# Turning the first batch's attention weights by TensorE's transpose mode, with x^T divided instead, and converting the float64 weights from one load

## The chip, the cores and the metric

The kernel runs on one core of a Trainium2 chip. The metric is the device time of one execution in microseconds (us). Seven runs of the kernel before gave a median of 1355.04 us, the lowest 1353.45 and the highest 1357.39.

## The reference: what is computed

Thresholded attention over 8 batches of 8 heads, 576 positions and head width 64, followed by a two-layer MLP with the exact gelu:

```python
scores = scale * np.matmul(q, k.transpose(0, 1, 3, 2))
thresh = np.max(scores, axis=-1, keepdims=True) - tau
scores = np.where(scores >= thresh, scores, -1000000000.0)
attn = np.exp(scores - np.max(scores, axis=-1, keepdims=True))
attn = attn / (np.sum(attn, axis=-1, keepdims=True) + 1e-09)
attn_out = np.matmul(attn, v)
x = attn_out.transpose(0, 2, 1, 3).reshape(B * S, H * D)       # 4608 tokens x 512
h = x @ w_in                                                   # 512 x 2048
out = (0.5 * h * (1.0 + erf(h / sqrt(2)))) @ w_out             # 2048 x 512
```

q, k and v are float32. The two weight matrices arrive as float64, so that each weight is two 32-bit words in memory; the kernel turns them into float32 itself.

## The kernel before, in words

Everything is one program on one core, with an order written out by hand; each engine runs its instructions in the order of the program, and an instruction waits for the data of other engines. TensorE is called PE, VectorE DVE, ScalarE ACT, GpSimd POOL, and the queue that issues most stores and some loads SP.

**Slots.** Attention is done for pairs of heads: 4 pairs in a batch, 32 in all. The rows of a pair's score matrix are taken in 5 chunks (four of 128 rows for each of the two heads, and one with the last 64 rows of both). One chunk of one pair is a *slot*. The first batch is slots 0 to 19: first chunks 0 and 1 of pairs 0 to 3 (slots 0 to 7), then chunks 2, 3 and 4 of pairs 0 to 3 (slots 8 to 19). In a slot PE makes the scores (`sc`, L403), DVE finds the row maximum (`nmx`, L415), POOL the threshold (`thr`, L416), ACT the exponential (`p`, L418), and DVE zeroes what lies under the threshold and sums the row (L434; the sum is `den`). The scores of the next slot use the same two PSUM rooms, so they wait for L434.

**The first batch (the change).** Its softmax weights p have to be transposed before they can meet v. `turn_p_early` (L335) does that on PE, one slot later, by an ordinary matmul against a diagonal matrix: `diagonal` (L440) takes the reciprocal of the sums on DVE (L445) and lets ACT scale the rows of an identity by it (`diag`, L448), and p^T diag(1/sum) (L345) is the transposed weights, already divided. ACT copies the result from PSUM (L353, L357, L364). A matmul of float32 is recorded as two matmul records and two weight-load records. `weigh_v` (L506) multiplies by v into x^T (L521), and ACT copies that to the blocks of x (`xall`, L531). In the first batch this happens in slots 3, 5, 7, 9 (the first 256 tokens of pairs 0 to 3) and 12, 15, 18, 21 (the other 320).

**The other batches** transpose p on DVE and by DMA, weigh it undivided, and divide x^T afterwards on POOL (`divide`, L545), by divisors that are spread over the partitions by DMA.

**Weights.** The float64 weights come in 32 pieces of 128 x 512 values (16 of w_in, then 16 of w_out). `load_piece` (L164) loads a piece twice, once as it is (`raw`, L186, 512 KB) and once starting three bytes later (`shifted`, L188), into rooms that are not yet in use for anything else: every other piece goes to one of the two halves of `turned_p`, the others to two free slots each of `xall`. The first two pieces are issued by SP, the rest by POOL, a new piece when one is done. `conversions` (L191) then takes for each piece four DVE instructions and one of ACT: the exponent bits of the high word (L207, DVE), rebiased (L208, ACT), 28 bits of the mantissa from the shifted copy (L215, DVE), the sign put to the exponent (L217, DVE), and the product of mantissa and power of two (L220, DVE). ACT is let run one piece ahead. `convert` spends a budget of DVE time on this, at the end of each slot (2000 ns in slots 1 and 2, 3800 ns in the later ones), with the costs that the `yield`s name, and at least one step ahead of L434 from slot 3 on.

**The MLP** works on blocks of 256 tokens: first layer `hT` (L597, 64 matmuls of 256 columns), gelu, second layer `o_ps` (L612, 32 matmuls of 512 columns). `fill` puts its matmuls between those of attention, as far as a list of goals (`GOAL`, in blocks, by slot) says and as weights are converted: 0 blocks until slot 9, rising to 0.42 by slot 19, to 1.92 by slot 43, and so on. Until slot 20 the results of the first layer are only copied to SBUF (L564), because gelu and exp need different tables of ACT; in slot 20 the gelus that have gathered run in one go (L570), between two table loads. The second layer needs them. The last ten blocks are done at the end by a different scheme (L785), without attention beside it.

Of the kernel before, what the change touches and what calls it, by code (L numbers as in the profile page):

```python
# [18 lines left out]
def kernel(  # L19
# [121 lines left out]
    rebias = const.tile([P, 1], FP32, name="rebias")  # L141
    nc.vector.memset(rebias, -8.0 * 896 * 2 ** 20)

# [20 lines left out]
    def load_piece(eng=nc.gpsimd):  # L164
        if loaded[0] == len(pieces):
            return
        k = loaded[0]
        if wide and len(x_free) < 2 and not (k % 2 and k < len(pieces) - LATER):
            return
# [7 lines left out]
        k = loaded[0] - 1  # L177
        slots = []
        if k % 2 and k < len(pieces) - LATER:

            room = pd[k // 2 % 2].bitcast(U32)
            raw, shifted = room[:, 0:2 * PIECE], room[:, 2 * PIECE:4 * PIECE]
        else:
            slots = [x_slot() for _ in range(2)]
            raw, shifted = (x_rows(i).bitcast(U32) for i in slots)
        eng.dma_start(raw, src.bitcast(U32))  # L186
        n = 8 * PIECE - 4
        eng.dma_start(shifted.bitcast(U8)[:, 0:n], src.bitcast(U8)[:, 3:3 + n])  # L188
        raws.append((dst, raw, shifted, slots))

    def conversions():  # L191
# [9 lines left out]
        while raws or ahead:  # L201
            if raws:
                dst, raw, shifted, slots = raws.pop(0)
                hi = raw.rearrange("p (f w) -> p f w", w=2)[:, :, 1]
                top = shifted.rearrange("p (f w) -> p f w", w=2)[:, :, 0]
                power = gp.tile([P, PIECE], U32, tag="g", name="power")
                vec.tensor_scalar(power, hi, 0x7FF00000, None, op0=ALU.bitwise_and)  # L207
                nc.scalar.activation(power, power, AF.Relu, bias=rebias, scale=8.0)  # L208
                ahead.append((dst, hi, top, dst.bitcast(U32), power, slots))
                yield 340  # L210
            if len(ahead) == LATER and converted[0] == len(pieces) - LATER:
                yield None
            if len(ahead) == 2 or not raws:
                dst, hi, top, mant, power, slots = ahead.pop(0)
                vec.tensor_scalar(mant, top, 0x0FFFFFFF, 0x10000000, op0=ALU.bitwise_and, op1=ALU.bitwise_or)  # L215
                yield 340
                vec.scalar_tensor_tensor(power, hi, 0x80000000, power, op0=ALU.bitwise_and, op1=ALU.bitwise_or)  # L217
                x_free.extend(slots)
                yield 720
                vec.scalar_tensor_tensor(dst, mant, 2.0 ** -28, power.bitcast(FP32), op0=ALU.mult, op1=ALU.mult)  # L220
                load_piece()
                converted[0] += 1
                yield 700
# [111 lines left out]
    def turn_p_early(p, i):  # L335
# [5 lines left out]
        w, diag = s.pop(("p", i)), s.pop(("diag", i))  # L341
# [702 lines left out]
    for n in range(len(slots) + WEIGH + 1):  # L1044
# [66 lines left out]
        if early:  # L1111
            diagonal(p, i)
# [53 lines left out]
```

## Time and profile before

| what | value |
|---|---|
| median of 7 runs | 1355.04 us |
| the profiled execution | 1354.34 us, its span 1352.6 us, 1.7 us around it |
| mean granted clock of PE over the span | 0.996 |
| first scores of slot 2, 10, 20, 21 | 16.88, 68.36, 136.24, 144.30 us |
| transposing matmuls of the first batch (L345) | 180, in 360 records |
| conversions (L207, L208, L215, L217, L220) | 32 of each |

The profile is of one execution. Busy times are shares of the span; matmuls overlap, and a matmul record of 275 ns can follow the one before it after 107 ns, so how many records pass in a stretch says more than the duration of one. The chain of work that ended last is followed back from the end: the work in it is what the time consists of. Windows give the busy time of every engine in a stretch, the clock granted to PE, and the share of the DMA engines' time in use.

### The profile page before, as it was taken

To read this page: it belongs to the slowest core of one execution; us is meant where nothing else is said; L and a number is where in the kernel's file an instruction comes from. 1 tells how busy PE (TensorE), PEld (TensorE's weight loads), DVE (VectorE), ACT (ScalarE), POOL (GpSimd) and SP (SyncE) were. 2 spreads that over 40 slices of the span, in tenths; PEclk is the share of its full clock that TensorE was granted. 3 is DMA by queue.
4 is the path that set the end of the run, shared out by engine and by line. 5 is a ranking of instruction groups with operands and counts; after the bars stand their busy time and mean duration, and the time that the engine had idled before them with its cause. 6 is when DMAs were issued, how large, how long until landed. Compare 5 with 4: busy or idle time off the path is not lost.

```text
span 1352.6 us, 20076 instructions
## 1 busy us (share of the span) xinstructions
PE 1333.7 (99%) x6398; PEld 904.6 (67%) x6398; DVE 1063.4 (79%) x2062; ACT 600.5 (44%) x1024; POOL 635.5 (47%) x1085
## 2 busy tenths in 40 slices
PE   9899999999999999999999999999999999999998
PEld 7677557457457457557557557568787787877877
DVE  6998677788888888888888888874758698385775
ACT  7766536447547528537637637413201112211120
POOL 5553344456555555554555552144363513625530
PEclk9999899999999999999999999999999999999999
DMA  9987366677777787787688777500000041000003
GB/s 291 329 299 235 76 155 147 145 156 185 158 176 184 155 197 181 156 212 174 152 206 182 153 172 160 117 9 1 0 1 0 12 114 32 1 1 0 1 0 78
DMA packets 212471, 169.18 MB, mean 125 GB/s; under 512 B 113872, under 2 KB 193600, under 8 KB 212368
## 3 DMA queue, kind: packets, MB, share of 16 engines
q1 hardware_dynamic: 188224, 112.53, 38.0%
q0 software_dynamic: 23712, 55.08, 13.2%
q8 instruction: 52, 0.85, 0.3%
q14 instruction: 51, 0.42, 0.1%
q10 hardware_dynamic: 432, 0.30, 0.1%
HBM read 72.73 MB, written 12.52 MB: 63 GB/s over the span
## 4 chain that ended last, share of the span: by engine, by line
PE 93%; DVE 3%; DMA 2%; ACT 1%; issue 1%; POOL 0%; SPq 0%; POOLq 0%; ACTq 0%; DVEq 0%
PE bank L785 34%; PE o_ps L612 17%; PE hT L597 16%; PE sc L403 13%; PE xT L521 11%; PE tr L345 1%; DMA v<-in_v_dram 1%; DVE nmx L415 1%; DVE p L434 1%; DMA xall<-in_moe_w_in_dram 1%; DVE power L217 1%; DMA k<-in_k_dram 0%; DVE w_in L220 0%; ACT p L418 0%; DVE power L207 0%
## 5 line engine op out<-in xcount | busy, mean ns | idle before, releaser
L418 ACT ACTIVATE p<-sc,nmx 128x576 f32<-128x576 f32 x288 | 201.7, 738 | 267.7 <-DVE nmx L415 267.3
L434 DVE SCALAR_TENSOR_TENSOR p<-sc,thr,p 128x576 f32<-128x576 f32 x288 | 225.4, 816 | 64.9 <-ACT p L418 60.2
L416 POOL TENSOR_SCALAR thr<-nmx,tau_eff 128x1 f32<-128x1 f32 x288 | 89.9, 312 | 374.4 <-DVE nmx L415 373.6
L415 DVE TENSOR_REDUCE nmx<-sc 128x1 f32<-128x576 f32 x288 | 205.1, 749 | 51.7 <-PE sc L403 50.6
L597 PE MATMUL hT<-xall,w_in 128*128 128x256 f32 x1024 | 241.9, 386 | 0.0
L612 PE MATMUL o_ps<-w_out,g 128*128 128x512 f32 x512 | 239.2, 607 | 0.0
L597 PEld LDWEIGHTS hT<-xall,w_in 128*128 128x128 f32 x1024 | 189.3, 190 | 51.0 <-issue 24.2
L667 DVE TENSOR_TENSOR c<-c,bank 128x320 f32<-128x320 f32 x304 | 147.1, 488 | 33.9 <-PE bank L785 20.6
L667 DVE TENSOR_TENSOR o<-o,bank 128x256 f32<-128x256 f32 x240 | 99.9, 420 | 93.7 <-PE bank L785 88.7
L612 PEld LDWEIGHTS o_ps<-w_out,g 128*128 128x128 f32 x512 | 93.9, 191 | 110.9 <-issue 108.5
L521 PE MATMUL xT<-pT,v 128*64 128x256 f32 (+1 forms) x1280 | 163.1, 409 | 0.0
L403 PE MATMUL sc<-kT,qT 64*128 64x288 f32 x960 | 159.1, 430 | 2.9 <-DVE p L434 2.3
L482 DVE STREAM_TRANSPOSE turned_p<-p 128x1152 f32<-128x1152 f32 x112 | 154.4, 1378 | 3.9
L403 PEld LDWEIGHTS sc<-kT,qT 64*128 64x128 f32 x960 | 91.2, 186 | 76.3 <-issue 63.2
L521 PEld LDWEIGHTS xT<-pT,v 128*64 128x64 f32 x1280 | 88.7, 137 | 71.9 <-issue 13.5
L785 PE MATMUL bank<-w_out,c 128*128 128x256 f32 x480 | 120.2, 381 | 0.5 <-DVE o L667 0.5
L265 POOL DMA_DIRECT2D v<-in_v_dram x208 | 111.3, 538 | 3.7 <-issue 1.8
L785 PEld LDWEIGHTS bank<-w_out,c 128*128 128x128 f32 x480 | 89.9, 190 | 18.8 <-DVE o L667 3.0
L838 ACT ACTIVATE c<-c 128x320 f32<-128x320 f32 (+1 forms) x80 | 46.9, 624 | 114.7 <-DVE c L667 114.6
L785 PE MATMUL bank<-t_out,c 128*128 128x256 f32 x320 | 82.8, 381 | 0.0
L667 POOL TENSOR_TENSOR c<-c,g 128x320 f32<-128x320 f32 (+1 forms) x40 | 50.6, 1273 | 67.5 <-DVE c L667 67.5
L785 PE MATMUL bank<-t_out,g 128*128 128x256 f32 x320 | 82.1, 379 | 0.0
(181 smaller groups left out, 1789.0 us busy)
## 6 DMA issues: line engine op xcount, KB each, us to landing
pT<-turned_p SPq DMA_DIRECT2D x448, 160.0 KB, 3.7
pT<-pd_tail SPq DMA_DIRECT2D x112, 80.0 KB, 3.0
q<-in_q_dram POOLq DMA_DIRECT2D x104, 72.0 KB, 3.0
k<-in_k_dram POOLq DMA_DIRECT2D x104, 72.0 KB, 3.4
inv<-turned SPq DMA_DIRECT2D x54, 128.0 KB, 3.9
v<-in_v_dram POOLq DMA_DIRECT2D x156, 40.0 KB, 3.2
out_dram<-o SPq DMA_DIRECT2D x40, 128.0 KB, 2.4
xall<-in_moe_w_out_dram POOLq DMA_DIRECT2D x9, 512.0 KB, 4.3
```

The lines of the kernel that those rows point to most:

```text
L265: eng.dma_start(t[r:P:4, e, 0:n, :], rows[:, r * KR:r * KR + n, :])
L403: nc.tensor.matmul(sc[e][:, h, 0:HALF], lhsT=lhsT, rhs=s["kT"][rows, at:at + HALF], start=True, stop=True)
L415: nc.vector.tensor_reduce(nmx[:, e:e + 1], sc, axis=AXIS.XY, op=ALU.max, negate=True)
L416: nc.gpsimd.tensor_scalar(thr[:, e:e + 1], nmx[:, e:e + 1], -1.0, tau_eff, op0=ALU.mult, op1=ALU.subtract)
L418: nc.scalar.activation(w[:, e * S:(e + 1) * S].rearrange("p (h s) -> p h s", h=2), sc, AF.Exp, bias=nmx[:, e:e + 1], scale=1.0)
L434: nc.vector.scalar_tensor_tensor(row, sc[e][:, :, 0:HALF], thr[:, e:e + 1], row, op0=ALU.is_ge, op1=ALU.mult, accum_out=den[e])
L482: nc.vector.transpose(turned_p[:, :, i // 2, 0:NB, i % 2 * Q:(i % 2 + 1) * Q], w.rearrange("p (e b i) -> p e b i", e=2, i=Q))
L521: nc.tensor.matmul(to, lhsT=s["v"][:, e, c, :], rhs=rhs, start=(c == 0), stop=(c == KR - 1))
L597: nc.tensor.matmul(hT[:, j % 2, :], lhsT=w_in_sb[c][:, j * P:(j + 1) * P], rhs=x_blk[n][:, c, :], start=(c == 0), stop=(c == N_DM - 1))
L612: nc.tensor.matmul(o[:, 0:d_model], lhsT=g[j][:, m * P:(m + 1) * P], rhs=w_out_sb[j], start=(j == 0), stop=(j == N_DF - 1))
L667: eng.tensor_tensor(out, a, b, op=ALU.add)
L785: nc.tensor.matmul(to, lhsT=l, rhs=r, start=start and k == 0, stop=k == len(pairs) - 1, skip_group_check=not start)
```

## The change

- The weights p of the first batch are transposed undivided, in TensorE's transpose mode against the identity. The 64 columns that are left of a chunk's two heads lie side by side, so that one transposition takes both: 9 for a full chunk instead of 8 large and 2 small matmuls, 5 for a last one.
- The reciprocal is still taken by DVE (`invert`). After x^T has been weighed, `divide_early` spreads the reciprocals over the partitions by small matmuls (the reciprocals, repeated 64 times, as the stationary operand against the identity), ACT copies them to SBUF, and POOL multiplies the blocks of x by them in place. ACT no longer makes `diag`.
- A piece of weights is loaded once. ACT makes two things of it: the high word, taken as a float32, times 2^-112, and the low word times 2^-29, written as an integer, which is its top 3 bits. DVE shifts the first left by 3 and masks it, puts in the sign, and adds the 3 bits as an integer. That is three DVE instructions and two of ACT for a piece. In the instruction list of the changed kernel the addition is a special instruction on 128 x 1024 elements of 16 bits.
- Four pieces are loaded by SP at the start instead of two, and two instead of one after slots 0 and 2, so that eight are on the way. The budget of `convert` is as before; the costs named for a piece sum to 1700 ns instead of 2100.
- The goal for slot 19 is 0.5 blocks instead of 0.42: all 64 first-layer matmuls of the first block stand ahead of slot 20, where 54 did.

```diff
     def load_piece(eng=nc.gpsimd):
...
-            room = pd[k // 2 % 2].bitcast(U32)
-            raw, shifted = room[:, 0:2 * PIECE], room[:, 2 * PIECE:4 * PIECE]
+            half, at = divmod(k // 2 % 4, 2)
+            raw = pd[half].bitcast(U32)[:, at * 2 * PIECE:(at + 1) * 2 * PIECE]
         else:
-            slots = [x_slot() for _ in range(2)]
-            raw, shifted = (x_rows(i).bitcast(U32) for i in slots)
+            slot = [x_slot()]
+            raw = x_rows(slot[0]).bitcast(U32)
         eng.dma_start(raw, src.bitcast(U32))
-        n = 8 * PIECE - 4
-        eng.dma_start(shifted.bitcast(U8)[:, 0:n], src.bitcast(U8)[:, 3:3 + n])
...
-                vec.tensor_scalar(power, hi, 0x7FF00000, None, op0=ALU.bitwise_and)
-                nc.scalar.activation(power, power, AF.Relu, bias=rebias, scale=8.0)
-                ahead.append((dst, hi, top, dst.bitcast(U32), power, slots))
-                yield 340
+                nc.scalar.activation(power.bitcast(FP32), hi.bitcast(FP32), AF.Copy, bias=0.0, scale=2.0 ** -112)
+                nc.scalar.activation(dst.bitcast(U32), lo, AF.Copy, bias=0.0, scale=2.0 ** -29)
+                ahead.append((dst, hi, power, slot))
+                yield 0
...
-                vec.tensor_scalar(mant, top, 0x0FFFFFFF, 0x10000000, op0=ALU.bitwise_and, op1=ALU.bitwise_or)
+                vec.tensor_scalar(power, power, 3, 0x7FFFFFF8, op0=ALU.logical_shift_left, op1=ALU.bitwise_and)
                 yield 340
                 vec.scalar_tensor_tensor(power, hi, 0x80000000, power, op0=ALU.bitwise_and, op1=ALU.bitwise_or)
...
-                vec.scalar_tensor_tensor(dst, mant, 2.0 ** -28, power.bitcast(FP32), op0=ALU.mult, op1=ALU.mult)
+                vec.tensor_tensor(dst.bitcast(U32), power, dst.bitcast(U32), op=ALU.add)
...
-        def turn(to, cols, e):
-            nc.tensor.matmul(to, lhsT=w[:, cols], rhs=diag[:, e, :], start=True, stop=True)
+        def turn(to, at):
+            nc.tensor.transpose(to, w[:, at:at + P], ident)
...
+        turn(tr[:, 0, :], MAIN if i < NC else S - P)
...
-    def diagonal(p, i):
+    def invert(p, i):
+        den = st[p]["sum", i]
+        nc.vector.reciprocal(den, den)
+
+    def divide_early(p, lo, hi):
         s = st[p]
-        den = s.pop(("sum", i))
-        n = den.shape[1]
-        nc.vector.reciprocal(den, den)
-        diag = s["diag", i] = dg.tile([P, 2, P], FP32, tag="inv", name="diag")
-        for e in range(n):
-            nc.scalar.activation(diag[:, e, :], ident, AF.Copy, bias=0.0, scale=den[:, e:e + 1])
+        b, hp = divmod(p, HP)
+        tr = ps.tile([P, 512], FP32, tag="mm", name="tr")
+        for i in range(lo // P, -(-hi // P)):
+            den = s.pop(("sum", i))
+            to = tr[:, i * P - lo:min((i + 1) * P, hi) - lo]
+            for e in range(2):
+                one_of, cols = (den[:, e:e + 1], ident) if i < NC else (den, ident[:, e * TAIL:(e + 1) * TAIL])
+                nc.tensor.matmul(to[e * D:(e + 1) * D, :], lhsT=one_of.to_broadcast([P, D]), rhs=cols, start=True, stop=True)
+        by = dg.tile([P, S], FP32, tag="inv", name="inv")
+        nc.scalar.copy(by[:, 0:hi - lo], tr[:, 0:hi - lo])
+        for n, o, at, size in in_blocks(b, lo, hi):
+            x, y = x_blk[n][:, hp, o:o + size], by[:, at - lo:at - lo + size]
+            ...
+            nc.gpsimd.tensor_tensor(x, x, y, op=ALU.mult)
...
-    for _ in range(2):
+    for _ in range(4):
         load_piece(nc.sync)
...
-    GOAL = [(-1, 0.0), (START - 1, 0.0), (BATCH - 1, 0.42)]
+    GOAL = [(-1, 0.0), (START - 1, 0.0), (BATCH - 1, 0.5)]
...
         for args in due:
             weigh_v(*args)
+            divide_early(*args)
...
         if p < 2 and i == 0:
-            load_piece()
+            for _ in range(2):
+                load_piece()
...
         if early:
-            diagonal(p, i)
+            invert(p, i)
```

## The prediction

> **What bounds the kernel now.** I read the page's shares and slices first, then the chain of waits, then windows and the timeline of the first 182 us, where the change lies.
>
> The page: busy time, and 40 slices of 34 us.
>
> ```profile
> PE 1333.7 (99%) x6398; PEld 904.6 (67%) x6398; DVE 1063.4 (79%) x2062; ACT 600.5 (44%) x1024; POOL 635.5 (47%) x1085
> ...
> PE   9899999999999999999999999999999999999998
> ...
> DVE  6998677788888888888888888874758698385775
> ```
>
> PE is the bound nearly everywhere; only in slices 2 and 3 is DVE as full. The change touches slices 1 to 5. So the question is what the first batch takes, and how far the MLP is by its end. Windows cut at the first scores of slots 2, 10, 20 and 26 (columns: length; busy time and instructions of PE, PEld, DVE, ACT, POOL; clock; DMA share; GB/s):
>
> ```profile
> 16.88:68.36 51.48, 45.42 (x387) 33.96 (x385) 50.12 (x113) 40.38 (x87) 27.38 (x53) 0.97 1.04 331
> 68.36:136.24 67.88, 65.55 (x405) 50.47 (x403) 61.49 (x136) 45.12 (x98) 31.48 (x59) 1.00 0.80 264
> 136.24:182.16 45.92, 44.32 (x156) 22.44 (x155) 32.01 (x59) 22.11 (x35) 16.67 (x39) 0.93 0.44 98
> 182.16:300.00 117.84, 117.84 (x581) 71.82 (x582) 91.82 (x165) 57.75 (x90) 59.53 (x120) 1.00 0.68 151
> ```
>
> Slots 2 to 9 are DVE's (50.1 of 51.5 us), slots 10 to 19 mostly PE's (65.6 of 67.9). From 182 us on PE has no gap: MLP work done earlier comes off there one for one. The chain by time shows what PE's slots consist of:
>
> ```profile
> 90.17 2.16 PE hT L597 x10
> 92.33 2.15 PE tr L345 x20
> 94.48 1.17 PE sc L403 x8
> ...
> 101.06 2.84 PE xT L521 x20
> ```
>
> So a record of hT takes 0.216 us (0.43 a matmul), one of the transposing matmul 0.107 (0.215 a matmul), a slot's scores 1.17 (1.08 with one room), a weighing 2.84. The timeline of one piece's conversion:
>
> ```profile
> 17.46 0.42 DVE L207 TENSOR_SCALAR power<-turned_p 128x512 uint32<-128x512 uint32 x1
> 17.58 1.33 ACT L208 ACTIVATE power<-power,rebias 128x512 uint32<-128x512 uint32 x2 [0.20 <-DVE power L207]
> 17.79 0.42 DVE L215 TENSOR_SCALAR w_in<-xall 128x512 uint32<-128x512 uint32 x1
> ...
> 18.33 0.69 DVE L217 SCALAR_TENSOR_TENSOR power<-xall,power 128x512 uint32<-128x512 uint32 x1
> ...
> 19.06 0.69 DVE L220 SCALAR_TENSOR_TENSOR w_in<-w_in,power 128x512 f32<-128x512 uint32 x1
> ...
> 19.66 0.16 DVE L445 RECIPROCAL den<-den 128x2 f32<-128x2 f32 x1
> ```
>
> From start to start DVE pays 0.33 for L207 and as much for L215 (17.46 to 17.79), 0.73 for L217, 0.60 for L220: 2.00 a piece. ACT pays about 0.62 for L208 (0.72 alone, 1.33 for two).
>
> **DVE, slots 2 to 9.** A piece now costs a one-source step (0.33 to 0.42, as it waits for ACT; nearest L207, I take 0.37), L217's form (0.73) and the addition. No row has that; 512 words at L220's rate are 0.60, 1024 elements one at a time, by the difference of L220 (0.69) and a 320-wide sum of two tensors on DVE (0.48, in the last blocks), cost 512 x 1.1 ns = 0.55 more, 1.15. I take 0.60, since the bytes are L220's: 1.70 a piece; the other end is 2.25. The Trainium skill (VectorE: DVE Perf Modes, What auto-detection actually checks) says that DVE takes two results a cycle where all operands are 16-bit with step 1, which these are, while two-source float32 stays at one; by it the addition lands at 0.60, and no run here shows it yet.
>
> The budget stays 3800 ns a slot while a piece is entered as 1700, not 2100, so more pieces are done per slot, not shorter slots. By the instruction list 18 are finished before slot 10's maximum, where the timeline before has 13. DVE work up to there: 50.1 - 13 x 2.00 + 18 x 1.70 = 54.7. Slot 10 starts 4.6 us *later*, and five more pieces are done.
>
> ACT in these slots: 40.4 - 13 x 0.62 (L208) + 18 x 2 x 0.62 - 15 diag of 0.34 + 3 copies of divisors of 0.35 = 50.6 of 56. It stays under DVE, but in slots 4 and 5 (three pieces, or a turn of q and k) it needs about 7 us for 6.4 of DVE. I put that at nothing, with an end of +3 for the range.
>
> **PE, slots 10 to 19.** Parts before: 6 x 1.17 + 4 x 1.08 scores = 11.3; 54 hT x 0.43 = 23.2; 172 records x 0.107 = 18.5; three weighings 8.5: 61.5 of 67.9, so 6.4 idle. After: 11.3; 64 hT 27.5; weighings 8.5; 78 transpositions; three spreads of the divisors. A transposition is 0.06 (one record, like the 64-column turns of q and k, 32 records in 1.97 us) to 0.215 (no gain): 4.7 to 16.8. I take 0.08, one record between 0.06 and 0.107: 6.2. A spread is 8 records at 0.06 and four small ones, 0.6: 1.9 in all (3.4 at 0.107). Sum 55.4. The Trainium skill (TensorE: Matmul & The Clock Gate, Part 4: PE-mode transpose) speaks against this: about 275 ns for a 128x128 transposition in a kernel, which moreover does not count as activity for the clock. By it, as an estimate, 78 x 0.275 is 21.5, not 6.2, and PE needs 70.7 instead of 55.4: the batch would end later than before. The trace has 275 ns as the *duration* of an L345 record, with 107 ns between two; I go by the spacing.
>
> DVE here: 61.5 - 19 x 2.00 + 14 x 1.70 = 47.3, and the conversions end in slot 16 instead of 19; ACT 45.1 - 18 x 0.62 - 18 x 0.34 + 14 x 1.24 + 3 x 0.4 = 46.4. PE stays the bound. Of its 6.4 idle, 2.0 (slot 18, waiting for a copy of ACT behind DVE's conversions) goes; slots 10 to 12, with seven pieces (19.6 us of DVE for 17.3 of PE), keep some. I leave 3.2, half: 58.6 instead of 67.9. Slot 20 starts at -9.3 + 4.6 = 4.7 us earlier. Ends: -9 (no idle but 1) to 0 (idle as before and ACT's +3).
>
> **Slot 20.** Before, PE had ten hT (4.3 us) to do while ACT ran exp, a table load and the gelus:
>
> ```profile
> 139.72 1.28 ACT L570 ACT_TABLE_LOAD   x1
> ...
> 141.02 3.23 ACT L570 ACTIVATE g<-g 128x512 f32<-128x512 f32 x6
> ...
> 143.34 1.02 PE L612 MATMUL o_ps<-w_out,g 128*128 128x512 f32 x2
> ...
> 144.30 1.24 PE L403 MATMUL sc<-kT,qT 64*128 64x288 f32 x8
> ```
>
> After, those are gone; a copy (0.58) stands ahead of the load, so the first gelu ends 5.9 us after the slot's scores, and five o_ps (0.9 each, 4.5) follow it ahead of slot 21's scores: 10.4 instead of 8.1, +2.3. PE idles 4.3 us there. Such a gap cost clock before:
>
> ```profile
> 54.00:57.00 3.00, 1.79 (x15) 0.94 (x13) 2.96 (x8) 2.00 (x5) 1.62 (x3) 1.00 1.00 383
> 57.00:60.00 3.00, 1.24 (x6) 1.24 (x7) 2.97 (x7) 1.93 (x5) 1.75 (x4) 0.72 1.08 333
> 60.00:63.00 3.00, 3.00 (x20) 2.66 (x21) 2.96 (x8) 1.63 (x5) 0.79 (x3) 0.71 1.00 393
> ```
>
> Six us at 0.71 lose 1.7; I enter 0.9, half. Against that four o_ps more are done by then, 3.6, which PE saves after 182 us.
>
> **What is entered at nothing, and its cover.** Loads: SP's four issues at the start carry the same bytes as before; POOL's fall from 60 to 28 (0.58 each, -18.6), for 8 multiplications of 0.73 and 4 of 0.32 (+7.1): POOL is half idle. DMA halves its 33.5 MB, but DVE waited 1.4 us in all for pieces (end -1.4). Waits added: the sums are now held until the spread has read them, in rooms of four, so in slots 12, 15 and 18 DVE's L434 waits for PE to finish weighing and spread (4.6 us after the slot's scores), and conversions queue behind it; L434 stood there 5.6 us after the scores (79.28 to 84.92), so the cover is DVE's own backlog; without it 1 to 2 us a time in PE's longest slots, +2. Exp of slot 2 stands behind three pieces on ACT, +0.6, inside the DVE sum. POOL's multiplication ahead of hT in slot 10 has a slot's time. At half clock PE's slots 7 and 9 are 9 us instead of 6: end +2.
>
> **Sum.** -4.7 (slots 2 to 19) + 2.3 + 0.9 (slot 20) - 3.6 (MLP ahead) = -5.1. From the profiled 1354.34, 0.7 under the median, to 1349.2; for the median 1350.
>
> **Rivals.**
> *ACT takes DVE's place.* With 7 us in slots 4 and 5 and conversions queued ahead of exp, DVE waits in L434: slots 2 to 9 longer by another 3 to 5 us, all else as above: 1353 to 1355. For it: 50.6 of 56 busy. Against it: ACT's idle before was DVE's doing (L208 waits for L207), and that wait is gone.
> *The addition goes element by element* (slower). At 1.15, 32 pieces cost 17.6 more on DVE; 18 of them lengthen slots 2 to 9 by 9.9, and the 14 others (7.7) reach 55.0 beside PE's 55.4, so most of the rest shows as well: +10 to +17, 1360 to 1367. It decides once a piece costs 0.28 more than entered (5.1 us over 18 pieces).
> *Transpositions cost what the matmuls did.* 0.215: +10.6 on PE in slots 10 to 19: 1355 to 1361, no gain or a small loss.
> *PE runs ahead better than entered*: idle 1, no clock loss, and the slots of DVE overlap with PE's: -9 + 2.3 - 3.6 - 1.4, 1343.
>
> **Numbers.** Mine with its ends (1346 to 1352.3) 0.46; PE ahead 0.17; ACT 0.20; addition 0.08; transposition 0.09. A difference under 0.2% (2.7 us) is about what a measurement can't tell from none. Faster: 0.46 + 0.17 = 0.63. ACT's case is the same, with a small part of transposition: 0.22. Slower 0.15. The range leaves out the addition's case and the far ends of the others: 1341 to 1358.
>
> **What would show it.** Right: slot 10 at about 73 us, slot 20 near 131.5; DVE over 0.95 in slots 2 to 9; one record a transposition, spaced 0.06 to 0.107; the last conversion in slot 16; PE idle some 4 us in slot 20, then a lower clock. Wrong if L434 waits for ACT's exp in slots 3 to 6, if the addition takes over 0.75, or if the clock is low through slots 10 to 19.

## The result, and the profile after

The changed kernel is slower: 1361.59 us in the median of 18 executions (1359.27 to 1364.04), beside 1355.06 in 43 for the kernel before. The ratio is 1.0046, with a 95% interval of 1.0038 to 1.0054. The forecast was 1350.0 in a range of 1341 to 1358, faster with a chance of 0.63: the sign is wrong and the time is outside the range. The profiled execution took 1362.96, its span 1361.2, at a mean clock of 0.989 (before: 1352.6 at 0.996).

First the page of the changed kernel: busy time, and slices of 34 us for PE and for PE's clock.

```profile
PE 1326.3 (97%) x6282; PEld 892.7 (66%) x6282; DVE 1055.9 (78%) x2029; ACT 605.3 (44%) x1027; POOL 619.7 (46%) x1065
...
PE   8789899999999999999999999999999999999998
...
PEclk9899899999999999999999999999999999999999
```

PE has 116 records less than before, and it is busy for 7 us less. But in slices 1, 2, 3 and 5 it is less full than before (8, 7, 8 and 8, where it had 9, 8, 9 and 9), and in slices 2 and 5 the clock is under 0.9 (before, in slice 5 alone). The change took work off PE, and PE did not use it.

The windows, cut at the first scores of slots 2, 10, 16, 20 and 21 (columns: length; busy time and instructions of PE, PEld, DVE, ACT, POOL; clock; DMA share; GB/s):

```profile
16.76:71.53 54.77, 42.99 (x329) 29.28 (x330) 51.66 (x106) 46.31 (x95) 23.52 (x46) 0.88 0.82 227
71.53:118.71 47.18, 42.10 (x230) 30.12 (x229) 38.59 (x80) 33.53 (x69) 16.03 (x31) 0.93 0.39 111
118.71:142.61 23.90, 23.36 (x141) 18.05 (x139) 14.70 (x32) 13.22 (x29) 4.34 (x13) 1.00 0.06 14
142.61:155.80 13.19, 9.19 (x24) 4.12 (x23) 5.46 (x11) 9.71 (x17) 1.34 (x8) 0.74 0.01 1
```

And slots 10 to 15 of the kernel before:

```profile
68.36:108.96 40.60, 40.31 (x248) 30.68 (x246) 37.67 (x83) 27.16 (x59) 22.94 (x42) 1.00 0.89 300
```

Against the same stretches of the kernel before (lengths in us):

| stretch | before | after | difference | forecast |
|---|---|---|---|---|
| slots 2 to 9 | 51.48 | 54.77 | +3.3 | +4.6 |
| slots 10 to 15 | 40.60 | 47.18 | +6.6 | -9.3 for both |
| slots 16 to 19 | 27.28 | 23.90 | -3.4 | |
| slot 20 | 8.06 | 13.19 | +5.1 | +3.2 |
| slots 21 and 22 | 12.38 | 12.94 | +0.6 | 0 |
| from slot 23 to the end | 1195.9 | 1192.5 | -3.5 | -3.6 |
| span (with -0.1 ahead of slot 2) | 1352.6 | 1361.2 | +8.6 | -5.1 |

So the question is slots 10 to 15 above all. DVE has about as much work there as before (38.6 us, 37.7 before). PE has fewer records (230, 248 before) and is busy with them for 42.1 us at a clock of 0.93, where it was 40.3 at 1.00. And yet these slots last 6.6 us longer. The chain that ended last shows two things in that stretch and in slot 20 (start, length, what):

```profile
86.78 4.10 PE xT L527 x20
...
109.59 4.53 PE xT L527 x20
...
130.45 2.84 PE xT L527 x20
...
148.54 7.33 PE o_ps L618 x10
```

The weighing of slot 18 takes 2.84 us (130.45), as all of them did before. Those of slots 12 and 15 take 4.10 and 4.53, and ten records of o_ps take 7.33 instead of 4.49. The windows of 3 us around the first and the last show why (the clock is the third figure from the end):

```profile
84.00:87.00 3.00, 2.53 (x10) 1.30 (x12) 2.93 (x8) 2.94 (x8) 0.84 (x3) 0.81 0.67 194
87.00:90.00 3.00, 3.00 (x16) 1.32 (x14) 2.86 (x6) 1.45 (x4) 1.22 (x3) 0.62 0.56 180
147.00:150.00 3.00, 1.46 (x2) 0.84 (x3) 2.55 (x7) 2.99 (x6) 0.00 (x0) 0.55 0.00 0
150.00:153.00 3.00, 3.00 (x5) 1.04 (x4) 0.00 (x0) 2.98 (x6) 0.00 (x0) 0.50 0.03 5
```

The granted clock is 0.81 and 0.62 in slot 12, and 0.55 and 0.50 in slot 20. Ahead of the first stands a wait of PE. PE's timeline, two rows (start, length, what, and in brackets how long PE sat idle before it and for whom):

```profile
77.97 1.21 PE L393 MATMUL sc<-kT,qT 64*128 64x288 f32 x6 [0.62 <-DVE p L424]
...
84.45 2.32 PE L393 MATMUL sc<-kT,qT 64*128 64x288 f32 x8 [1.95 <-DVE p L424]
```

The scores of slot 12 wait 1.95 us for L424, which frees their PSUM rooms. And DVE's timeline shows what L424 waited behind:

```profile
78.53 0.43 DVE L209 TENSOR_SCALAR power<-power 128x512 uint32<-128x512 uint32 x1
78.99 0.69 DVE L211 SCALAR_TENSOR_TENSOR power<-turned_p,power 128x512 uint32<-128x512 uint32 x1
79.82 0.69 DVE L214 CUSTOM_DVE_ANT_0 w_out<-power,w_out 128x1024 uint16<-128x1024 uint16 x1
80.43 0.42 DVE L209 TENSOR_SCALAR power<-power 128x512 uint32<-128x512 uint32 x1
80.89 0.69 DVE L211 SCALAR_TENSOR_TENSOR power<-xall,power 128x512 uint32<-128x512 uint32 x1
...
81.57 1.40 DVE L405 TENSOR_REDUCE nmx<-sc 128x1 f32<-128x576 f32 x2
82.89 0.68 DVE L214 CUSTOM_DVE_ANT_0 w_out<-power,w_out 128x1024 uint16<-128x1024 uint16 x1
83.48 0.81 DVE L424 SCALAR_TENSOR_TENSOR p<-sc,thr,p 128x576 f32<-128x576 f32 x1
```

The scores of slot 11 were all there at 79.2 us (77.97 + 1.21). Their maximum (`nmx`, L405) starts only at 81.57, since conversions stand ahead of it on DVE: five instructions from 78.53 on, L209 and L211 and L214 of one piece and the first two of the next. L424 (83.48) follows the maximum, the exponential and one more L214. So here PE's wait is made by the conversions on DVE.

### The profile page after: what moved, and what is told of

Same layout as the page of the kernel before. It is cut to its first block, busy times and chain, and to the rows that moved or that the text cites. A ratio compares the mean times of both kernels' runs of the same rounds, so it can differ in the third digit from the quotient of the medians.

```text
span 1361.2 us, 19815 instructions
## 1 busy us (share of the span) xinstructions
PE 1326.3 (97%) x6282; PEld 892.7 (66%) x6282; DVE 1055.9 (78%) x2029; ACT 605.3 (44%) x1027; POOL 619.7 (46%) x1065
## 4 chain that ended last, share of the span: by engine, by line
PE 88%; DVE 5%; DMA 3%; ACT 2%; issue 1%; SPq 1%; POOL 0%; DVEq 0%; ACTq 0%
PE bank L791 33%; PE o_ps L618 16%; PE hT L603 15%; PE sc L393 12%; PE xT L527 10%; DVE nmx L405 1%; DMA q<-in_q_dram 1%; DVE p L424 1%; DVE power L211 1%; DMA x<-xall 1%; ACT p L408 1%; DVE power L209 1%; ACT pT L346 0%; PE tr L339 0%; DMA turned_p<-in_moe_w_in_dram 0%
## 5 line engine op out<-in xcount | busy, mean ns | idle before, releaser
L424 DVE SCALAR_TENSOR_TENSOR p<-sc,thr,p 128x576 f32<-128x576 f32 x288 | 225.3, 815 | 68.2 <-ACT p L408 64.8
L405 DVE TENSOR_REDUCE nmx<-sc 128x1 f32<-128x576 f32 x288 | 205.1, 749 | 56.2 <-PE sc L393 55.2
L393 PE MATMUL sc<-kT,qT 64*128 64x288 f32 x960 | 162.0, 430 | 10.1 <-DVE p L424 9.4
L527 PE MATMUL xT<-pT,v 128*64 128x256 f32 (+1 forms) x1280 | 168.7, 417 | 0.3
L488 DVE STREAM_TRANSPOSE turned_p<-p 128x1152 f32<-128x1152 f32 x112 | 154.4, 1378 | 3.9
```

Of the source, the lines that this page charges most:

```text
L393: nc.tensor.matmul(sc[e][:, h, 0:HALF], lhsT=lhsT, rhs=s["kT"][rows, at:at + HALF], start=True, stop=True)
L405: nc.vector.tensor_reduce(nmx[:, e:e + 1], sc, axis=AXIS.XY, op=ALU.max, negate=True)
L424: nc.vector.scalar_tensor_tensor(row, sc[e][:, :, 0:HALF], thr[:, e:e + 1], row, op0=ALU.is_ge, op1=ALU.mult, accum_out=den[e])
L488: nc.vector.transpose(turned_p[:, :, i // 2, 0:NB, i % 2 * Q:(i % 2 + 1) * Q], w.rearrange("p (e b i) -> p e b i", e=2, i=Q))
L527: nc.tensor.matmul(to, lhsT=s["v"][:, e, c, :], rhs=rhs, start=(c == 0), stop=(c == KR - 1))
```

## The experiments

From this I had a first theory: PE has less work, waits for 2 to 4 us, its clock is halved just behind each wait, and that is the loss. The rivals: the wait in slot 20 alone; the conversions; the later division. Ratios below are to the kernel before, with 95% intervals. The stretches named are those of the profiled executions.

### The goal put back

```diff
-    GOAL = [(-1, 0.0), (START - 1, 0.0), (BATCH - 1, 0.5)]
+    GOAL = [(-1, 0.0), (START - 1, 0.0), (BATCH - 1, 0.42)]
```

> The changed kernel with one number put back: the goal for slot 19 is 0.42 blocks again, so that ten hT matmuls (4.3 us) stand in slot 20 as before. Theory (the first batch leaves PE waiting, and after a wait of some 2 to 4 us the granted clock is halved for the next 6 us, in slots 7 to 9, 12, 15 and in slot 20): only the loss of slot 20 goes. Slot 20 falls from 13.2 us to 8 to 9, o_ps x10 from 7.33 to 4.5, against four o_ps fewer ahead (3.6); slots 10 to 19 are up to 4 us shorter where PE bounds them, and less where it does not: 1356 to 1360, the low clock in slots 12 and 15 stays. Rival (slot 20 is the whole loss): 1355 or less. Rival (conversions or the divided x^T cost it): 1361 to 1362, as the changed kernel.

Measured: 1361.8 us, ratio 1.0045 (1.003 to 1.0061), the same as the changed kernel. PE's timeline of slot 20:

```profile
141.31 4.48 PE L603 MATMUL hT<-xall,w_in 128*128 128x256 f32 x20
146.21 1.10 PE L618 MATMUL o_ps<-w_out,g 128*128 128x512 f32 x2 [0.41 <-DVE pT L350]
```

The wait in slot 20 is filled by ten hT matmuls and the slot lasts 7.71 us. The profiled execution took 1358.55 us, one of the two shortest of six. Beside that of the changed kernel it gains 5.5 us in slot 20 and 3.8 in slots 10 to 19, and loses 4.2 from slot 21 on, by the MLP work that is no longer ahead (from slot 23 on it takes 1195.1 us instead of 1192.5). It also loses 1.9 in slots 2 to 9, although their instructions are the same in both kernels: 56.7 us at a clock of 0.82 here, 54.8 at 0.88 there. So much differs from execution to execution. The other four executions lie between 1361.7 and 1364.1 us, with a clock of 0.987 or 0.988, and no profile shows where they lose it. The goal alone takes nothing off the median, and the theory's 1356 to 1360 was too low.

### The conversions alone, and the turning alone

`new_conversion` is the kernel before with `load_piece`, `conversions` and the four early loads of the changed kernel. `new_turning` is the changed kernel with those of the kernel before, and the goal of 0.42.

> The kernel before with the new conversions alone: one load for a piece, three DVE and two ACT instructions, four pieces at the start; turning against the divided identity and the goal of 0.42 as before. Theory (clock): PE keeps the 18.5 us of turning in slots 10 to 19, so its waits there stay short and the clock stays at 1.00: 1352 to 1357. Rival (the conversions cost it: ACT has some 55 us of work in the 51 to 56 us of slots 2 to 9, DVE waits for it): 1359 to 1364, with slots 2 to 9 over 56 us.

> The kernel before with the new turning alone: transpose mode, x^T divided by spread reciprocals; conversions from two loads and the goal of 0.42 as before. Theory (clock): DVE keeps its 2.00 us a piece, PE has 10 us less to do in slots 10 to 19, so PE waits more and the clock is halved after the waits, in slots 12, 15 and 18 above all: 1358 to 1365, slots 10 to 19 not below 66 us. Rival (the conversions cost it): 1348 to 1353, since PE's lighter work shows at last. Rival (dividing x^T later costs it by its waits, whatever the clock): 1358 to 1365 at a clock near 1.00.

Measured: conversions alone 1361.48 us, ratio 1.004 (1.0027 to 1.0052); turning alone 1357.43 us, ratio 1.0021 (1.0008 to 1.0034), between its theory and its first rival. The conversions alone cost as much as the whole change, so the time is that of the rival, though slots 2 to 9 last 54.5 us, not over 56. The profiled execution of `new_conversion` has a clock of 0.999, and is the fastest of its kernel at 1357.83 (the others: 1360.2 to 1362.1 at 0.994 to 0.995). Even so its span is 3.5 us longer than that of the kernel before: the clock can't be the whole cause. Its windows for slots 10 to 15 and 16 to 19:

```profile
70.10:114.60 44.50, 41.44 (x248) 30.35 (x247) 38.10 (x80) 35.70 (x76) 12.97 (x26) 1.00 0.44 118
114.60:139.54 24.94, 24.94 (x158) 19.81 (x156) 14.72 (x32) 15.01 (x35) 3.40 (x11) 1.00 0.05 13
```

Slots 10 to 15 last 44.5 us at a full clock, 3.9 longer than before, with DVE busy for 38.1 of them. Slots 10 to 15 of `new_turning`:

```profile
70.77:111.27 40.50, 36.05 (x218) 26.71 (x217) 38.20 (x82) 24.86 (x52) 25.46 (x46) 1.00 0.83 298
```

Here slots 10 to 15 are as before (40.50) although PE has 36.05 us of work instead of 40.31: DVE, with 38.2, is what bounds them. PE's lighter work does not show, and the clock is lower in the stretches beside it (0.87 in slots 2 to 9, 0.88 in 16 to 19).

### Does more work on PE hold the clock?

```diff
-            nc.tensor.transpose(to, w[:, at:at + P], ident)
+            nc.tensor.matmul(to, lhsT=w[:, at:at + P], rhs=ident, start=True, stop=True)
```

> The changed kernel with the transpositions made by an ordinary matmul against the identity: two records of 0.107 instead of one of 0.109, so 164 x 0.106 = 17.4 us more for PE, 8.3 of it in slots 10 to 19. Theory (clock): the added work fills waits, the clock in slots 2 to 19 rises from 0.88 and 0.95 to near 1.00, and the time is no longer than the changed kernel's: 1356 to 1362. Rival (PE's work is what counts, the low clock is chance or costs little): 1366 to 1372.

Measured: 1368.45 us, ratio 1.0097 (1.0084 to 1.011). Of 17.4 us of added work 6.9 show, and the clock stays at 0.990 to 0.992 with the waits for L424 still there (2.7 us in slots 10 to 19, 5.1 in slots 2 to 9). Work spread over all slots does not fill the few long waits. The rival's 1366 to 1372 held. So transpose mode itself was worth about 7 us to the changed kernel.

### The pace of the conversions

What the new conversions change in time is the number of pieces in a slot: the budget of 3800 ns was kept, while a piece's named costs fell from 2100 to 1700. By the counts of the last DVE instruction of a piece, the kernel before finishes 13 pieces ahead of slot 10, 12 in slots 10 to 15 and 7 in slots 16 to 19; the changed kernel 16, 14 and 2. The budget is cut in the same proportion, in `new_conversion` and in the changed kernel:

```diff
-        convert(0 if n == 0 else 2000 if n < 3 else 3800 if n < BATCH - 1 else 1e9)
+        convert(0 if n == 0 else 1600 if n < 3 else 3080 if n < BATCH - 1 else 1e9)
```

> The kernel before with the new conversions (as in new_conversion), and the budget cut by what a piece's named costs fell, 1700 to 2100: 1600 instead of 2000 ns in slots 1 and 2, 3080 instead of 3800 from slot 3 on, so that some 13 pieces are done by slot 10 as before, not 18. Theory (the conversions alone cost 6 us because they put five more pieces into slots 2 to 9, which DVE and ACT bound, and PE's slots 10 to 19 have no use for what that takes off them): slots 2 to 9 last 48 to 51 us instead of 54.5, slots 10 to 19 67 to 69: 1350 to 1356. Rival (it is ACT: two instructions of 0.6 us a piece stand ahead of diag, and PE waits for diag, whatever the pace): 1359 to 1362, PE's waits for diag still 7 us and more in slots 2 to 9.

> The changed kernel with the same cut of the budget (1600 and 3080 ns). Theory (pace): slots 2 to 9 fall from 54.8 to 50 to 52 us and PE waits less for L424 there, so the clock holds better: 1354 to 1358. Rival (the pace has no part in it; the low clock and slot 20 have): 1360 to 1363. Rival (the conversions then take from slots 14 to 19 what they gave to slots 2 to 9): slots 10 to 19 over 74 us, 1360 and more.

Measured: `conversion_paced` 1352.91 us, ratio 0.9982 (0.9972 to 0.9992); `after_paced` 1354.32 us, ratio 0.9992 (0.9984 to 1.0001). One line takes the conversions from 0.4% slower to 0.2% faster than before, and the changed kernel from 1.0046 to a tie. (The profiled executions of `new_conversion` and `conversion_paced` differ by 4.5 us, the medians by 8.6.) The windows of `conversion_paced`, slots 10 to 15 and 16 to 19:

```profile
68.60:110.10 41.50, 40.63 (x248) 30.59 (x246) 34.50 (x73) 32.05 (x70) 15.40 (x29) 1.00 0.53 151
110.10:136.18 26.08, 25.59 (x159) 19.74 (x157) 21.75 (x46) 21.51 (x47) 5.16 (x11) 1.00 0.10 31
```

13 pieces are finished ahead of them, 12 and 6 in them. DVE has 34.5 us of work in the first instead of 38.1, and it is 41.5 instead of 44.5 us long; slots 2 to 9 are 2.3 shorter (52.2, where 48 to 51 had been expected), slots 16 to 19 1.1 longer. In `after_paced` slots 10 to 15 and 16 to 19 are:

```profile
68.36:108.93 40.57, 38.43 (x230) 29.03 (x229) 35.40 (x71) 30.22 (x63) 17.82 (x34) 1.00 0.54 153
108.93:134.30 25.37, 24.29 (x140) 18.35 (x138) 20.94 (x45) 20.14 (x41) 5.94 (x13) 1.00 0.12 34
```

65.9 us together, at a clock of 1.00, where the changed kernel had 71.1. Slots 2 to 9 last 53.0, more than the 50 to 52 expected.

### The pace in slots 10 to 19 alone

```diff
-        convert(0 if n == 0 else 2000 if n < 3 else 3800 if n < BATCH - 1 else 1e9)
+        convert(0 if n == 0 else 2000 if n < 3 else 3800 if n < 10 else 2400 if n < BATCH - 1 else 1e9)
```

> The changed kernel with the budget cut in the later slots alone: 2000 and 3800 ns up to slot 9 as in the changed kernel, 2400 instead of 3800 ns from slot 10 on, so that the last 14 pieces are spread over slots 10 to 19 instead of standing in 10 to 15. Theory (in slots 10 to 15 two and three pieces a slot make DVE's L424 late, PE waits, and the clock falls in the weighing behind the wait): slots 2 to 9 last 54 to 55 us as in the changed kernel, slots 10 to 19 fall from 71.1 to 65 to 67 with no low clock in slots 12 and 15: 1355.5 to 1358. Rival (it is what slots 2 to 9 hold that decides): slots 10 to 19 over 69, 1359.5 to 1362.

Measured: 1357.28 us, ratio 1.0016 (1.0007 to 1.0025), some 4 us less than the changed kernel. DVE's timeline in slot 11, to be held beside that of the changed kernel:

```profile
80.50 0.43 DVE L209 TENSOR_SCALAR power<-power 128x512 uint32<-128x512 uint32 x1
80.96 0.69 DVE L211 SCALAR_TENSOR_TENSOR power<-turned_p,power 128x512 uint32<-128x512 uint32 x1
...
81.64 1.40 DVE L405 TENSOR_REDUCE nmx<-sc 128x1 f32<-128x576 f32 x2
```

One piece less stands between the two slots' L424 and the maximum (three instructions fewer), the scores of slot 12 follow without a wait (at 84.53), and the weighing behind them takes 2.74 us from its start to that of the spread (86.40 to 89.14), 4.00 in the changed kernel. The windows of slots 10 to 15 and 16 to 19:

```profile
73.72:112.80 39.08, 38.22 (x231) 28.90 (x230) 32.02 (x67) 28.83 (x61) 16.07 (x31) 1.00 0.47 130
112.80:138.21 25.41, 23.16 (x141) 17.68 (x139) 18.32 (x39) 17.93 (x37) 5.18 (x13) 1.00 0.06 14
```

Ten pieces instead of 14 are in the first, and it lasts 39.1 instead of 47.2 us: 8.1 less, for 6.6 less of DVE's work. PE is busy for 38.2 of it, so now it is PE's. This shows the cause of the loss in slots 10 to 15: the number of pieces in them. (That it is not the clock, which also rose, the next run shows.) Slots 2 to 9, whose instructions are those of the changed kernel, last 57.3 here, at a clock of 0.82; the theory had 54 to 55. That takes back part of the 6.6 us which slots 10 to 19 gain in this execution.

### The clock held

`clock_held` is the changed kernel with matmuls that compute nothing, placed where PE waits; `n` is the slot.

```diff
+    KEEP = {7: 8, 9: 7, 12: 4, 15: 3}
...
+        if n in KEEP:
+            keep = ps.tile([P, 2 * P], FP32, tag="mm", name="keep")
+            for _ in range(KEEP[n]):
+                nc.tensor.matmul(keep, lhsT=ident, rhs=w_in_sb[0][:, 0:2 * P], start=True, stop=True)
...
         if n == BATCH:
             gelus_held()
+            keep = ps.tile([P, 2 * P], FP32, tag="mm", name="keep")
+            for _ in range(9):
+                nc.tensor.matmul(keep, lhsT=ident, rhs=w_in_sb[0][:, 0:2 * P], start=True, stop=True)
```

> The changed kernel with matmuls of 128 x 256 that compute nothing, put on PE where it waited in the profile of the changed kernel: 8, 7, 4 and 3 of them (0.43 us each) ahead of the scores of slots 7, 9, 12 and 15, which wait for DVE's L424 there, and 9 behind those of slot 20, where the second layer waits for the gelus. Theory (clock): the waits are filled, PE never idles over 1 us there, the granted clock stays at 1.00; xT x20 of slots 12 and 15 takes 2.84 again instead of 4.10 and 4.53, o_ps x10 4.5 instead of 7.33, the mean clock goes from 0.989 to 0.995: 1354 to 1358. Rival (the low clock costs little, for PE waits afterwards anyhow): 1360 to 1363 at a clock of 0.995. Rival (added work on PE is added time): 1363 to 1370.

Measured: 1358.32 us, ratio 1.0022 (1.0013 to 1.0031), at 0.995 to 0.999, just over the theory's 1354 to 1358: 31 matmuls that compute nothing make the changed kernel some 3 us faster. The windows of slots 2 to 9, 10 to 19 and 20:

```profile
15.85:70.70 54.85, 47.04 (x358) 32.76 (x359) 51.36 (x106) 46.22 (x95) 23.71 (x45) 0.97 0.84 232
70.70:140.79 70.09, 64.19 (x381) 48.94 (x381) 53.56 (x112) 47.07 (x98) 20.64 (x44) 1.00 0.28 81
140.79:151.22 10.43, 10.36 (x43) 6.45 (x42) 5.49 (x11) 9.12 (x16) 1.35 (x8) 1.00 0.01 2
```

It says where the low clock costs. Slots 10 to 15 hold 14 pieces here too, and they still last 46.2 us (70.70 to 116.90) at a clock of 1.00, where `late_paced` with ten pieces had 39.1: there the pieces cost, and hardly the clock. Slots 10 to 19 together fall by 1.0 only, to 70.1. Slot 20 falls from 13.19 to 10.43, since PE has no slack there. For slots 2 to 9 it leaves the price open: they last 54.85 us, as in the profile of the changed kernel (54.77 at 0.88), but the same slots without the added matmuls took 56.7 and 57.3 at 0.82 in `goal_042` and `late_paced`.

In slots 12 and 15 the added matmuls come late. PE's timeline ahead of the scores of slot 12:

```profile
83.86 1.99 PE L1058 MATMUL keep<-w_in,ident 128*128 128x256 f32 x8 [1.83 <-ACT pT L350]
```

PE still waits 1.83 us, now for a copy of ACT (ahead of slot 15, 1.40), and then has the added matmuls to do before the scores. So the 1.0 us is what a full clock gave less what the matmuls cost.

### Was it transpose mode that let the clock fall?

```diff
-            nc.tensor.transpose(to, w[:, at:at + P], ident)
+            for _ in range(2):
+                nc.tensor.transpose(to, w[:, at:at + P], ident)
```

> The changed kernel with every transposition issued twice into the same place, in transpose mode: PE has the same added time as in turn_by_matmul (164 x 0.109 = 17.9 us), but of the other kind. If the clock follows PE's waits whatever the kind of work: as turn_by_matmul, 1366 to 1371, mean clock 0.990 to 0.992, low in the same places (slots 7, 9, 12, 20). If transpose mode is no activity for the clock: a lower clock than in turn_by_matmul, 0.980 to 0.987, low also in slots where PE does nothing but transpose and wait for a few us, and 1371 to 1378.

Measured: 1365.78 us, ratio 1.0082 (1.0068 to 1.0095), beside 1.0097 (1.0084 to 1.011) of `turn_by_matmul`, with a clock of 0.992 to 0.995. Slots 10 to 19 of `turn_by_matmul`:

```profile
73.94:150.06 76.12, 72.69 (x446) 57.73 (x444) 52.13 (x109) 47.45 (x97) 19.30 (x43) 0.96 0.26 72
```

And of `turned_twice`:

```profile
73.37:145.79 72.42, 69.47 (x447) 55.22 (x445) 53.78 (x112) 47.54 (x98) 20.54 (x44) 1.00 0.28 79
```

Added transpositions keep the clock at least as well as added matmuls of the same time (1.00 and 0.96), and the 1371 to 1378 us at 0.980 to 0.987 that were expected if they did not are far off. The Trainium skill (TensorE: Matmul & The Clock Gate, Part 4: PE-mode transpose) states that transpose mode does not count as PE being busy in the same way; these two runs speak against it, though in none did PE have nothing but transpositions to do.

### Pace and clock together

`paced_goal_042` is `after_paced` with the goal of 0.42. `paced_goal_held` adds to that the empty matmuls ahead of slots 7 (8) and 9 (3). `paced_held_20` is `after_paced`, goal 0.5, with those and the 9 in slot 20.

> The changed kernel with both numbers put back in proportion: the budget of 1600 and 3080 ns (as in after_paced) and the goal of 0.42. Theory (in after_paced PE waits 4.3 us for the gelus in slot 20, because the ten hT that stood there before are done earlier): the wait is filled, slot 20 falls from 12.4 us to 8 to 8.5, slots 10 to 19 lose up to 4.3 us of hT, and four o_ps (3.6) come off the MLP done ahead: 3 to 5 us less than after_paced, 1349 to 1352, and at or under conversion_paced. Rival (what slot 20 gains is taken back, as between the changed kernel and goal_042): 1353.5 to 1355.5.

> As paced_goal_042, with matmuls that compute nothing ahead of the scores of slot 7 (8, 3.4 us) and of slot 9 (3, 1.3 us), where PE waited 3.35 and 1.53 us for L424 in after_paced and the clock was 0.50 to 0.59 afterwards. Theory (clock): no low clock from 48 to 57 us, the weighing of slot 7 takes 2.6 instead of 4.4; slots 2 to 9 end 1 to 2 us earlier than in paced_goal_042, and the time falls by as much: 1347 to 1351. Rival (DVE bounds slots 2 to 9, PE's clock there costs nothing): the same time as paced_goal_042 within 1 us, with the clock at 1.00 there.

> The changed kernel (goal 0.5) with the budget of 1600 and 3080 ns and the empty matmuls ahead of the scores of slots 7 (8) and 9 (3) and behind those of slot 20 (9, 3.9 us, where PE waits 4.3 us for the gelus). Theory: what pace and clock gave apart comes together: 1354.3 of after_paced less 1.6 (what slots 7 and 9 gave in paced_goal_held) less 1.7 (o_ps x10 in slot 20 6.25 to 4.5): 1349 to 1352.5, under both kernels and under conversion_paced (1352.9). Rival (what slot 20 gains comes back later): 1352.5 to 1354.

Measured: 1354.58 us, ratio 0.9995 (0.9983 to 1.0006); 1352.98, ratio 0.9981 (0.9971 to 0.9991); 1350.38, ratio 0.9966 (0.9954 to 0.9979). The goal makes no difference a second time: its rival held. The matmuls ahead of slots 7 and 9 are worth 1.6 us between the medians of one chip (the intervals overlap; 1347 to 1351 had been expected). In the profiles slots 2 to 9 last 50.7 us with them in `paced_goal_held` and 50.6 in `paced_held_20`, and 54.2 and 53.0 without them in `paced_goal_042` and `after_paced`. PE's timeline of slot 7 in `after_paced`, behind a wait of 3.35 us:

```profile
48.34 3.00 PE L393 MATMUL sc<-pd_tail,qT 64*128 64x288 f32 x8 [3.35 <-DVE p L424]
51.27 4.38 PE L527 MATMUL xT<-pT,v 128*64 128x256 f32 x20
```

And in `paced_held_20`, with the wait filled:

```profile
45.36 3.62 PE L1058 MATMUL keep<-w_in,ident 128*128 128x256 f32 x16
...
50.74 2.38 PE L527 MATMUL xT<-pT,v 128*64 128x256 f32 x20
```

The weighing falls from 4.38 to 2.38 us. Slot 20 of the same kernel:

```profile
134.14 4.15 PE L1072 MATMUL keep<-w_in,ident 128*128 128x256 f32 x18
...
139.22 4.56 PE L618 MATMUL o_ps<-w_out,g 128*128 128x512 f32 x10 [0.37 <-ACT g L576]
```

Ten records of o_ps take 4.56 instead of 6.25 us in `after_paced`. This kernel is faster than the one before by 0.34%, and than the changed one by some 11 us, with matmuls in it that compute nothing. Useful work in those places might do better, which was not tried.

The stretches side by side, in us; for pieces those finished ahead of slot 10, in slots 10 to 15, and in 16 to 19:

| kernel | pieces | slots 2-9 | 10-15 | DVE busy there | 16-19 | slot 20 | median |
|---|---|---|---|---|---|---|---|
| before | 13, 12, 7 | 51.5 | 40.6 | 37.7 | 27.3 | 8.1 | 1355.1 |
| after | 16, 14, 2 | 54.8 | 47.2 | 38.6 | 23.9 | 13.2 | 1361.6 |
| new_conversion | 16, 14, 2 | 54.5 | 44.5 | 38.1 | 24.9 | 8.0 | 1361.5 |
| late_paced | 17, 10, 5 | 57.3 | 39.1 | 32.0 | 25.4 | 13.6 | 1357.3 |
| conversion_paced | 13, 12, 6 | 52.2 | 41.5 | 34.5 | 26.1 | 8.3 | 1352.9 |
| after_paced | 13, 12, 6 | 53.0 | 40.6 | 35.4 | 25.4 | 12.4 | 1354.3 |
| paced_held_20 | 13, 12, 6 | 50.6 | 41.1 | 35.9 | 25.3 | 10.7 | 1350.4 |

## Why the prediction was wrong, by its own steps

**DVE, slots 2 to 9: the limit right, the size partly luck.** The forecast had slot 10 at about 73 us; it is at 71.53. DVE is busy for 51.7 of 54.8 us, where the forecast had 54.7 of work and no idle. Its 18 pieces were counted to slot 10's maximum, and 18 are finished by then; but the 13 of the kernel before were counted to slot 10's first scores, and by those the changed kernel has finished 16. So two pieces too many stood in the sum, and 3.1 us of idle, put at nothing, made up for them (1.7 of it waits for ACT's conversions). The addition took 0.69 us, with the next instruction 0.60 behind it, so 0.60 was the right one of 0.60 and 1.15. The rule of the Trainium skill (VectorE: DVE Perf Modes, What auto-detection actually checks), that operands of 16 bit with step 1 go two a cycle, agrees with the 0.60 of this trace.

**A transposition: mis-sized, small.** I took 0.08 between 0.06 and 0.215. It is one record and follows the one before after 0.109 us (nine in 0.98), though each is recorded with some 0.28. So 78 of them cost 8.5, not 6.2: +2.3. The Trainium skill's 275 ns (TensorE: Matmul & The Clock Gate, Part 4: PE-mode transpose) is near the recorded duration, and not what a transposition adds to PE's time here.

**PE, slots 10 to 19: the step that failed.** "Of its 6.4 idle, 2.0 goes; I leave 3.2, half: 58.6 instead of 67.9." It is 71.1, that is 55.4 + 2.3 for the transpositions + 13.4 idle and lost clock. Three things are in the 13.4:
- The halving had no ground: with the pieces spread and the clock at 1.00, `late_paced` still lasts 64.5 in these slots, 6.8 over the parts (57.7), about as much as the 6.4 before. Of these the profiles name 2.9 us as waits of PE, and 2.2 before, most of them for copies of ACT; what the rest is made of is not shown.
- The pieces: 5.6 us, as what is left (13.4 - 6.8 - 1.0). I compared DVE's 47.3 with PE's 55.4 over all ten slots and called the stretch PE's. But the budget puts 14 of the 16 remaining pieces into slots 10 to 15, where DVE has 38.6 us of work and waits for 5.9 (3.3 of it for ACT's two conversions, 1.4 for PE's spread of the divisors, 1.2 for POOL and for a copy of ACT), and leaves 2 for slots 16 to 19, where PE is busy for 23.4 of 23.9. The working itself had "19.6 us of DVE for 17.3 of PE" for slots 10 to 12, and then took an average over it.
- The clock: 1.0, by `clock_held`, net of the matmuls added there.

DVE's waits in slots 10 to 15 of the changed kernel (us in total, times, the longest):

```profile
DVE power L209 <- ACT power L201: 3.3, 2, 2.4
DVE p L424 <- PE tr L446: 1.4, 1, 1.4
DVE p L424 <- ACT g L570: 0.7, 1, 0.7
DVE den L433 <- POOL den L427: 0.5, 1, 0.5
```

In the kernel before these waits sum to 2.3 (1.3 for ACT's L208). So of the 6.6 us that slots 10 to 15 lost, 0.9 is more work of DVE and 3.6 are more waits of DVE, above all for ACT, which has two instructions to do for a piece where it had one; the profile names nothing for the remaining 2.1. `late_paced` still has 5.5 us of such waits there: what it takes out of these slots is DVE's work, 6.6 us. What the waits alone cost, no run separates.

So the gain from cheaper pieces was spent on bringing them forward, into slots that DVE and its waits set: +3.3 in slots 2 to 9 and +6.6 in 10 to 15, against -3.4 in 16 to 19.

**Slot 20: mechanism right, size off.** +2.3 for the wait on the gelus and +0.9 for the clock were entered; +5.1 was measured. The wait is 4.0 us (4.3 forecast). The clock was at 0.50 to 0.55 behind it, and o_ps x10 took 7.33 instead of 4.49: 2.8, where 0.9 had been entered, half of what six us at 0.71 lose. That 0.71 was an average over windows: cut finely, the clock of the kernel before is 0.50 from 58.34 to 61.74 us and 1.00 on both sides. And its profile has a second dip, from 157 to 164 us behind a wait of 1.58 us, which the prediction did not use:

```profile
159.00:162.00 3.00, 3.00 (x5) 1.17 (x4) 2.74 (x7) 0.87 (x2) 0.44 (x2) 0.50 0.24 51
```

**MLP ahead: right, the closeness partly luck.** -3.6 was entered; from slot 23 on -3.5 was measured. But that stretch of the kernel before holds the dip at 157 us, and that of the changed kernel has none. Beside `goal_042`, which has the old goal and no dip there either, it is 1192.5 against 1195.1: -2.6.

**Entered at nothing.** That sums are held until they are spread made L424 wait 1.4 us once in slots 10 to 15, so the cover named for it (DVE's backlog) did not hold in full; the end of +2 did. POOL and the loads cost next to nothing that shows (0.5 us of DVE's waits in those slots are for POOL).

**The rivals.** None of the four is what happened. ACT taking DVE's place came nearest: DVE does wait for ACT's conversions, but 1.7 us in slots 2 to 9 and 3.3 in 10 to 15. The low clock stood in an end of +2 for slots 7 and 9 and in the last sentence, "if the clock is low through slots 10 to 19", there without a price. The pace stood nowhere as a rival, though its cause (3800 ns kept, 1700 named) was in the text.

**The ends.** Those of slots 2 to 19 do not follow from their terms: "no idle but 1" gives 55.4 + 1 - 67.9 + 4.6 = -6.9, not -9, and idle as before with ACT's +3 gives +1.5, not 0.

**The whole.** Against the 6.5 us of the loss (medians), pacing the pieces takes back 7.3, holding the clock 3.3, both together some 11. That both together end at 1350.4, close to the forecast, is partly chance: slots 10 to 19 are 66.4 us there, not 58.6, and the gain lies in slots 2 to 9, which the forecast had at 56.1 and which are 50.6.

**What stays open.** The turning alone is at 1.0021, although PE has some 15 us less to do in the first batch (360 records of 0.107, less 164 of 0.109 and eight spreads of 0.6 to 0.7); the clock of its executions (0.990 to 0.992 in most, 0.995 before) fits a loss of that kind, but no run held the clock in that kernel. The profiled execution of `new_conversion` shows 3.5 of its 6.1 us; the rest is in executions at a lower clock, of which there is no profile.

## What to carry to other kernels

When a cheaper step is scheduled by a budget with named costs, the kernel does not get its time back: it does more of the step per slot, and in slots that the same engine bounds this makes each of them longer; cut the budget with the cost. Sum a stage where its limit is one and the same: an average over ten slots called the stretch PE's, when six of them were DVE's and four PE's. And taking work off PE pays only where PE was the last to finish; elsewhere it turns into waits, and a wait of a few us can lower the clock for the work behind it (4.00 us of waiting ahead of o_ps x10 in slot 20, which then took 7.33 us instead of 4.49), which costs where that work is on the path.

## What was not expected of the hardware

- Waits of 1.3 to 2 us can be enough, and are not always. In the changed kernel PE waited 1.95 us ahead of slot 12 and 1.32 ahead of slot 15, and the weighings behind them took 4.10 and 4.53 us instead of 2.84. The Trainium skill (TensorE: Matmul & The Clock Gate, Part 1: What's actually happening) speaks of an idle window of about 3.4 us; these waits are shorter. In `clock_held`, waits of 1.83 and 1.40 us in the same places, with added matmuls behind them, left the clock at 1.00.
- The clock does not always fall behind the longest wait. In slot 6 of the changed kernel it was at 0.50 from 45 us on, ahead of the wait of 3.15 us that ended at 50.80; the wait before that was one of 1.50, up to 43.31.
- Executions differ: `after_paced` has the same program in each execution, and they lie between 1352.96 us at a clock of 0.995 and 1355.53 at 0.993, with 0.990 among them; `goal_042` lies between 1358.14 at 0.994 and 1364.06 at 0.987. The Trainium skill (TensorE: Matmul & The Clock Gate, Part 1: What's actually happening) says that the window runs freely, without regard to the program's start, which would make such differences. What the profiles show of it is the length of the low clock: cut finely, it is 0.50 from 85.90 to 89.30 us in slot 12 of the changed kernel, 3.4 us, from 147.33 to 154.14 in slot 20, twice that, and from 44.93 to 55.17 from slot 6 on, three times that.
- Empty work shortened the time: 31 matmuls took 3 us off the changed kernel, the 20 of `paced_held_20` some 4 off `after_paced` (3.5 by the ratios).
